# One-token attention: scores as rows with the query columns as weights, two value tiles in one accumulator, and 20 wide output rows

## The chip, the core and the metric

The kernel runs on one core of a Trainium2 chip. Its engines work side by side and wait for each other only through semaphores: TensorE (PE, with its weight loads listed as PEld), VectorE (DVE), ScalarE (ACT), GpSimd (POOL), and SyncE (SP), which here only issues transfers. PE writes into PSUM, a small memory of eight banks of 128 partitions x 512 f32 values; the other data lie in SBUF (128 partitions). The metric is the device time in microseconds of one execution. The kernel before took 189.35 us (median of 3 runs, 189.26 to 189.45).

## The reference

One token `x` (512 values) goes through two branches, mixed by a gate:

```python
g = sigmoid((x * gate_w).sum(-1))
# branch A: attention, 32 heads, 4096 cached keys and values of 128 values each
q = (x @ wq) as 32 heads of 128
p = softmax(einsum("hd,hkd->hk", q, k_cache) * 128 ** -0.5)
a = einsum("hk,hkd->hd", p, v_cache).reshape(4096) @ wo      # wo: 4096 x 512
# branch B: an MLP with 1376 hidden units
b = relu(x @ w1 + b1) ** 2 @ w2 + b2
out = g * a + (1 - g) * b                                     # 512 values
```

Everything is bf16. Keys and values are 33.6 MB each, wq and wo 4.2 MB each, w1 and w2 1.4 MB each: 78.3 MB that are read once.

## The kernel before

**Tiles.** Four heads make a tile; there are `NQ` = 8 tiles. A key tile is loaded as 128 partitions of 128 keys: partitions 32h to 32h+31 hold head h of the four, each partition 128 consecutive keys of its head. A value tile has the same layout. Three buffers hold keys (`Kt`), two hold values (`Vt`); the last two value tiles go into key buffers, wo into a value buffer.

**Transfers.** All large ones are issued by SP, in one queue and in this order: wq, K0, w1, w2, K1, V0, K2, K3, V1, K4, V2 and so on to V6, V7, and wo in four pieces of 20, 8, 3 and 1 rows (`TS`; a row is 128 of the 4096 inputs times 512 outputs). Where a buffer is used again the issue waits for its last reader: K2 goes where w1 and w2 were and waits for the MLP's last product (`s_ml`, line 258); K3 on waits for the transposes (`s_t`), DVE's products (`s_mu`) and POOL's products (`s_pm`) of an older tile; values wait for the value products (`s_pv`). The output leaves at the end.

**Scores.** The 128 keys in each partition of a tile are shared out among three engines:

- 68 go to POOL, in four pieces of 17 (line 310): keys times the query, which lies broadcast in `qb`, into `pg` (two buffers); DVE sums each piece (`psums`, line 691).
- 28 go to DVE alone, in two pieces of 14: `prods` (line 676) and `sums` (line 685).
- 32 go to PE, in four chunks of 8 (`TC`). `transposes(i, c)` (line 423) turns 8 blocks of 128x128 keys into a PSUM bank (`T`, three of them), `evac` on ACT (line 338) copies them to `kT`, and `scores(i, c)` (line 437) makes one product for each block: the turned keys are the weights, four query columns `qc` stream. PE issues the transposes two chunks ahead of the scores. At the end of a tile ACT copies the scores from `pS` into the score tile `Sb`, head by head (`score_copy`, line 344).

**Softmax of a tile.** DVE's `smax(i)` (line 698) takes the maximum of each partition, PE turns that column into a row (`max_rows`, 447), DVE's `gmax` (702) takes the maximum of each head, PE spreads it (`max_cols`, 451), ACT negates it (`neg_max`, 348) and makes the exponentials (`exps`, 355), which write `E`, four columns for each key block, zero outside the head's own partitions.

**Values.** `pv(i, a, b)` (line 466) makes 32 products for a tile: 16 columns of `E` (4 key blocks x 4 heads) are the weights and 4 x 128 value columns stream. They go round four column groups of the array, accumulators at partitions 0, 32, 64 and 96 of `pO`. After each tile `pv_copy` (ACT, line 361) copies 112 partitions of `pO` to `pvf`, and `extract(i)` (line 475) adds up what belongs to each head with the 0/1 matrix `pick`, into `O`.

**Order.** Each engine's order is written out by hand. PE, for tile i: transposes and scores of i; in tile 0 then the MLP (`mlp_h`, `mlp_c`, `mlp_out`); in tile 1 `mlp_cols`; then `max_rows(i-1)`, `extract(i-3)`, the first half of `pv(i-2)`, `max_cols(i-1)`, the second half. DVE, for tile i: `prods(i,0)`, `psums(i-1,3)`, `smax(i-1)`, `psums(i,0)`, `sums(i,0)`, `gmax(i-1)`, `psums(i,1)`, `prods(i,1)`, the next query, `psums(i,2)`, in tile 0 the MLP's two instructions (`mlp()`, lines 707 and 709), `sums(i,1)`.

**MLP.** `mlp_h` (lines 495 and 498) streams the bias and w1 (5 x 1376 columns) past one weight column into the three `T` banks; ACT copies the row (375); `mlp_c` (506) turns it into columns, and adds 1 to `s_h`, for which DVE's `mlp()` waits; `mlp_out` (516, 524) multiplies by w2.

**End.** After tile 7: `extract(5)`, `pv(6)`, `max_rows(7)`, `max_cols(7)`, `extract(6)`, then `busy(n)`: products whose result nobody uses, which fill PE's waits (line 569), two of them, one after each of three exponentials, the denominator (`den`, 482), five more, `pv(7)`, a copy by DVE (735), `extract(7)`, the scaling (738), `regroup` (537, 740), two more fillers, and the wo rows (`attn_rows`): 16 (`WW`) of the first piece's 20 are wide, 512 columns in four column groups of `pO` (547); DVE copies them to `pvf` (742), `wide_rows` (562) adds them up; the other rows are four products of 128 columns each (553).

Of the kernel before, what the change touches and what calls it, by code (L numbers as in the profile page):

```python
# [5 lines left out]
def bass_gated_mix__gqa_block_cached__dense_activation_squared_relu__decode_kernel(  # L6
# [21 lines left out]
    NH = 32  # L28
# [34 lines left out]
    NT = 3  # L63
    NR = 3
# [6 lines left out]
    WW = 16  # L71
# [12 lines left out]
    with ctx:  # L84
# [26 lines left out]
        xrow = sb("xrow", [1, DM], bf16)  # L111
        grow = sb("grow", [1, DM], bf16)
        b1r = sb("b1r", [1, F], bf16)
# [9 lines left out]
        pick = sb("pick", [128, 4, 60], fp32)  # L123
        pvf = sb("pvf", [112, 512], fp32)
        onesf = sb("onesf", [1, 128], fp32)
        qc = sb("qc", [128, NH], bf16)
        Sb = sb("Sb", [128, NS, NB], fp32)
        E = sb("E", [128, NE, NB, 4], bf16)
# [16 lines left out]
        b2r = Kt[0:1, 2, 14 * 1024:14 * 1024 + DM]  # L145
        b2g = Kt[0:1, 2, 15 * 1024:16 * 1024].bitcast(fp32)

        pick2 = sb("pick2", [112, 3], fp32)
# [13 lines left out]
        SL = pS[0:NH, 0:256].bitcast(bf16)  # L162
        H = pX[:, 160:160 + FN + TX]
# [9 lines left out]

        S = pS[:, 0:4 * max(YB)].rearrange("p (b h) -> p b h", h=4)

# [43 lines left out]
        s_sd = sem("s_sd")  # L219
        s_cp = sem("s_cp")  # L220
# [95 lines left out]
        def _(eng):  # L316
# [9 lines left out]
            for j in QA:  # L326
# [6 lines left out]
            eng.activation(qc[:, :].rearrange("p (j h) -> p j h", h=4), QT[:, :, 0:128:HP], ACT.Copy)\  # L333
               .then_inc(s_qc, 1)

            def evac(n):
                eng.wait_ge(s_t, n + 1)
                eng.activation(kT[:, n % NR, :], T[n % NT][:, :].bitcast(bf16), ACT.Copy).then_inc(s_ev, 1)  # L338
# [12 lines left out]
            def exps(j):  # L351
                eng.wait_ge(s_nm, j + 1)
                for h in range(4):
                    a, b = HP * h, HP * h + HP
                    eng.activation(E[a:b, j % NE, :, h], Sb[a:b, j % NS, :], ACT.Exp,  # L355
                                   bias=nM[a:b, 4 * j + h:4 * j + h + 1], scale=SCALE,
                                   accum_out=RS[a:b, 4 * j + h:4 * j + h + 1]).then_inc(s_e, 1)

            def pv_copy(j):
                eng.wait_ge(s_pv, j + 1)  # L360
                eng.activation(pvf[:, :], pO[0:112, :], ACT.Copy).then_inc(s_pc, 1)  # L361

            for i in range(NQ + 1):
                if i == NQ:
                    pv_copy(NQ - 3)
                    pv_copy(NQ - 2)
                if i < NQ:
                    for c in range(NC[i]):
                        evac(CB[i] + c)
                        if c == 1 and i >= 3:  # L370
                            pv_copy(i - 3)
                    score_copy(i)
                    if i == 0:
                        eng.wait_ge(s_h, 1)
                        eng.activation(hrow, TT[0:1, 0:F], ACT.Copy).then_inc(s_hw, 1)
                        eng.wait_ge(s_ml, 1)
                        eng.activation(pvf[:, :], pO[0:112, :], ACT.Copy).then_inc(s_mc, 1)
                if i >= 1:
                    neg_max(i - 1)
                    exps(i - 1)  # L380
# [4 lines left out]
        def _(eng):  # L385
# [29 lines left out]
            def transposes(i, c):  # L415
                n = CB[i] + c
                if c == 0:
                    eng.wait_ge(s_k[i % NK], 16 * (i // NK + 1))
                if n >= NT:
                    eng.wait_ge(s_ev, n - NT + 1)  # L420
                for y in range(TC):
                    w = XB[i] + c * TC + y
                    mm = eng.transpose(T[n % NT][:, :].bitcast(bf16)[:, y * 128:(y + 1) * 128],  # L423
                                       Kt[:, i % NK, w * 128:(w + 1) * 128], ident[:, :])
                mm.then_inc(s_t, 1)

            def scores(i, c):
                n = CB[i] + c
                eng.wait_ge(s_ev, n + 1)
                if c == 0:  # L430
                    if i == 0:
                        eng.wait_ge(s_qc, 1)
                        eng.wait_ge(s_g, 3)
                    else:
                        eng.wait_ge(s_cp, 4 * i)
# [19 lines left out]
            def pv(i, a, b):  # L455
                if a == 0:
# [5 lines left out]
                    if i >= 1:  # L462
                        eng.wait_ge(s_pc, i)
                for y in range(a, b):
                    r = 32 * (y % 4)
                    mm = eng.matmul(pO[r:r + 16, :], E[:, i % NE, 4 * y:4 * y + 4, :],  # L466
                                    VT(i)[:, y * 512:(y + 1) * 512], start=(y < 4), stop=(y >= NG - 4))
# [4 lines left out]
            def extract(i):  # L472
                eng.wait_ge(s_pc, i + 1)
                for b in range(4):
                    mm = eng.matmul(O, pick[0:112, b, 28 - 4 * i:60 - 4 * i], pvf[:, b * 128:(b + 1) * 128],  # L475
                                    start=False, stop=(i == NQ - 1 and b == 3), skip_group_check=True)
# [25 lines left out]
            def mlp_c():  # L502
                eng.wait_ge(s_hw, 1)
                eng.wait_ge(s_ho, 9)
# [4 lines left out]
            def mlp_out():  # L509
# [3 lines left out]
                eng.wait_ge(s_wm, 3)  # L513
# [14 lines left out]
            def mlp_cols():  # L528
                eng.wait_ge(s_mc, 1)
                for j in range(4):  # L530
                    eng.matmul(accs[j % 2], pick2[:, 1 - j // 2:3 - j // 2], pvf[0:112, j * 128:j * 128 + 128],
# [40 lines left out]
            for i in range(NQ):  # L572
                for c in range(NC[i]):
                    transposes(i, c)
                    if c >= 2:
                        scores(i, c - 2)
                scores(i, NC[i] - 2)
                scores(i, NC[i] - 1)
                if i == 0:
# [7 lines left out]
                if i >= 3:  # L587
                    extract(i - 3)
# [6 lines left out]
            extract(NQ - 3)  # L595
# [3 lines left out]
            extract(NQ - 2)  # L599
# [8 lines left out]
            extract(NQ - 1)  # L608
# [10 lines left out]
        def _(eng):  # L619
# [8 lines left out]
            eng.tensor_reduce(pick[:, :, 28:32],  # L628
                              identf[:, :].rearrange("p (c r) -> p c r", c=4)[:, :, 0:16]
                              .rearrange("p c (b h) -> p b h c", b=4), AX.X, ALU.add).then_inc(s_ho, 1)  # L630
# [3 lines left out]
            eng.wait_ge(s_ho, 7)  # L634
            eng.wait_ge(s_wm, 2)
            eng.tensor_copy(pick2[:, 1:2], pick[0:112, 0, 28:29]).then_inc(s_wm, 1)
# [98 lines left out]
            eng.tensor_copy(pvf[:, :], pO[0:112, :]).then_inc(s_pc, 1)  # L735
            eng.wait_ge(s_rd, 1)
            eng.wait_ge(s_ex, NQ)
# [4 lines left out]
            eng.tensor_copy(pvf[:, :], pO[0:112, :]).then_inc(s_wc, 1)  # L742
# [30 lines left out]
```

## Time and profile before

| what | value |
|---|---|
| runs (median of 3) | 189.35 us |
| span of the profiled execution | 188.1 us |
| median less span | 1.25 us |
| transfers | 78.48 MB, mean 417 GB/s |
| mean granted PE clock | 0.701 |
| one POOL piece (L310) | 4.32 us, 32 of them |
| DVE per tile: sums of POOL's pieces (L691), its own products (L676) and sums (L685) | 4 x 2.41, 2 x 2.01, 2 x 2.00 us |
| first key tile used by POOL, last POOL piece over | 22.8 us, 167.1 us |
| last wo piece issued, output issued | 151.0 us, 186.9 us |

The profile is one execution. Times in the time line are microseconds from the start of the span; a line gives start, duration, engine, line of the kernel, operation, output <- input, shapes, and in brackets the idle time before it and what ended that. The lines called windows give, for a stretch, the busy time of each engine (with the number of instructions), the granted PE clock (1.00 is full), the busy share of the transfer engines and their rate.

### The profile page before, as it was taken

Reading aid. Unit: us, or ns where it says so; the run is one execution under the profiler, and the core shown is the slowest. Engines: PE = TensorE matmul, PEld = TensorE weight load, DVE = VectorE, ACT = ScalarE, POOL = GpSimd, SP = SyncE. Lnnn points to the kernel's source line nnn. Section 1 sums busy time; section 2 is a strip of 40 time slices with the busy share of each in tenths; the row PEclk is TensorE's granted clock in tenths of the full one; section 3 lists DMA queues with packets and bytes.
Section 4 is the critical chain, followed back from the end, with each engine's and each line's share of the span. In section 5 each row is a group of like instructions: output and inputs, shape, how many; then the busy total and the mean of one; then the engine's idle time right before and its main releaser. Section 6 shows DMA issues by size and latency. Waiting matters only on the chain. (4 is left out here: it accounts for less than half of the span.)

```text
span 188.1 us, 2610 instructions
## 1 busy us (share of the span) xinstructions
PE 109.1 (58%) x1076; PEld 65.3 (35%) x1078; DVE 153.0 (81%) x127; ACT 69.6 (37%) x170; POOL 137.8 (73%) x38
## 2 busy tenths in 40 slices
PE   1129877788302839147506571758185649458986
PEld 0113253428202716133403171418141634214334
DVE  5122569999997999999999999999999999992022
ACT  2102476208320819403920573055405460505000
POOL 1000199998995999989998999899899989950000
PEclk9999999555755756657955866555855556755799
DMA  6999899999999999999999999999999999999993
GB/s 223 447 446 446 380 440 446 432 439 432 429 441 432 413 425 429 432 439 439 429 418 432 432 432 429 439 439 418 425 436 432 432 432 432 442 411 420 433 393 124
DMA packets 3374, 78.48 MB, mean 417 GB/s; under 512 B 394, under 2 KB 527, under 8 KB 676
## 3 DMA queue, kind: packets, MB, share of 16 engines
q1 hardware_dynamic: 3356, 78.32, 97.4%
q8 instruction: 8, 0.13, 0.3%
q14 instruction: 2, 0.02, 0.0%
q10 hardware_dynamic: 8, 0.01, 0.0%
HBM read 78.33 MB, written 0.00 MB: 416 GB/s over the span
## 5 line engine op out<-in xcount | busy, mean ns | idle before, releaser
L310 POOL TENSOR_TENSOR pg<-Kt,qb 128x2176 f32<-128x2176 bf16 x32 | 137.1, 4318 | 28.5 <-DMA Kt<-in_A_k_cache_dram 23.6
L691 DVE TENSOR_REDUCE Sb<-pg 128x17 f32<-128x2176 f32 x32 | 77.0, 2405 | 1.7 <-POOL pg L310 1.7
L338 ACT ACTIVATE kT<-T 128x1024 bf16<-128x1024 bf16 x32 | 30.8, 1030 | 16.7 <-PE T L423 16.5
L423 PE MATMUL T<-ident,Kt 128*128 128x128 bf16 x256 | 25.6, 280 | 18.2 <-DMA Kt<-in_A_k_cache_dram 18.2
L676 DVE TENSOR_TENSOR pr<-Kt,pQ 128x1792 f32<-128x1792 bf16 x16 | 32.2, 2011 | 2.1 <-DMA Kt<-in_A_k_cache_dram 1.3
L685 DVE TENSOR_REDUCE Sb<-pr 128x14 f32<-128x1792 f32 x16 | 32.1, 2004 | 0.0
L423 PEld LDWEIGHTS T<-ident,Kt 128*128 128x128 bf16 x256 | 22.4, 130 | 22.8 <-DMA Kt<-in_A_k_cache_dram 21.1
L466 PE MATMUL pO<-Vt,E 128*16 128x512 bf16 x192 | 21.8, 543 | 0.2 <-issue 0.2
L348 ACT ACTIVATE nM<-pM 128x4 f32<-128x4 f32 x8 | 1.4, 173 | 47.5 <-PE pM L451 47.5
L355 ACT ACTIVATE E<-Sb,nM 32x128 bf16<-32x128 f32 x32 | 18.6, 580 | 0.9
L437 PE MATMUL pS<-qc,kT 128*128 128x4 bf16 x256 | 11.7, 167 | 10.2 <-ACT kT L338 9.9
L475 PE MATMUL pX<-pvf,pick 112*32 112x128 f32 x64 | 14.5, 403 | 2.4 <-ACT pvf L361 2.4
L447 PE MATMUL pM<-identf,mp 128*1 128x128 f32 x8 | 2.8, 347 | 20.3 <-DVE mp L698 20.3
L437 PEld LDWEIGHTS pS<-qc,kT 128*128 128x128 bf16 x256 | 9.9, 102 | 12.3 <-ACT kT L338 12.2
L408 PE MATMUL T<-Vt,kT 128*128 128x512 bf16 x32 | 10.7, 484 | 3.4 <-DMA Vt<-in_A_wq_dram 3.4
L475 PEld LDWEIGHTS pX<-pvf,pick 112*32 112x32 f32 x64 | 9.5, 161 | 6.1 <-ACT pvf L361 2.9
L330 ACT ACTIVATE qb<-T 32x128 bf16<-32x128 f32 x20 | 5.4, 268 | 10.5 <-PE T L408 10.2
L663 DVE CAST qb<-T 32x128 bf16<-32x128 f32 x12 | 3.4, 287 | 6.5 <-PE T L408 6.2
L466 PEld LDWEIGHTS pO<-Vt,E 128*16 128x16 bf16 x192 | 6.4, 104 | 6.2 <-issue 4.0
L451 PE MATMUL pM<-gm,onesf 1*128 1x4 f32 x16 | 4.1, 325 | 7.4 <-DVE gm L702 7.2
L447 PEld LDWEIGHTS pM<-identf,mp 128*1 128x1 f32 x8 | 0.6, 79 | 21.8 <-DVE mp L698 21.6
L355 ACT ACTIVATION_READ_ACCUMULATOR E<-Sb,nM 32x1 f32 x32 | 8.1, 254 | 0.0
(81 smaller groups left out, 76.8 us busy)
## 6 DMA issues: line engine op xcount, KB each, us to landing
Kt<-in_A_k_cache_dram SPq DMA_DIRECT2D x8, 4096.0 KB, 31.0
Vt<-in_A_v_cache_dram SPq DMA_DIRECT2D x6, 4096.0 KB, 31.3
Kt<-in_A_v_cache_dram SPq DMA_DIRECT2D x2, 4096.0 KB, 31.3
Vt<-in_A_wq_dram SPq DMA_DIRECT2D x1, 4096.0 KB, 12.3
Vt<-in_A_wo_dram SPq DMA_DIRECT2D x1, 2560.0 KB, 32.9
Kt<-in_B_w_dram SPq DMA_DIRECT2D x1, 1376.0 KB, 24.4
Kt<-in_B_w_dram SPq DMA_DIRECT2D x1, 1280.0 KB
Vt<-in_A_wo_dram SPq DMA_DIRECT2D x1, 1024.0 KB, 34.9
```

The lines of the kernel that those rows point to most:

```text
L310: eng.tensor_tensor(pg[:, n % 2, 0:g, :], Kt[:, i % NK, k * g * 128:(k + 1) * g * 128] .rearrange("p (b d) -> p b d", b=g), qb[:, i:i + 1, ...
L330: eng.activation(qb[a:b, j, :], T[j % NT][a:b, h * 128:(h + 1) * 128], ACT.Copy)\
L338: eng.activation(kT[:, n % NR, :], T[n % NT][:, :].bitcast(bf16), ACT.Copy).then_inc(s_ev, 1)
L355: eng.activation(E[a:b, j % NE, :, h], Sb[a:b, j % NS, :], ACT.Exp, bias=nM[a:b, 4 * j + h:4 * j + h + 1], scale=SCALE, accum_out=RS[a:b, ...
L408: mm = eng.matmul(T[j % NT][:, :], xb[:, t, :], wq_sb[:, t, j * 512:(j + 1) * 512], start=(t == 0), stop=(t == 3))
L423: mm = eng.transpose(T[n % NT][:, :].bitcast(bf16)[:, y * 128:(y + 1) * 128], Kt[:, i % NK, w * 128:(w + 1) * 128], ident[:, :])
L437: mm = eng.matmul(S[:, c * TC + y, :], kT[:, n % NR, y * 128:(y + 1) * 128], qc[:, 4 * i:4 * i + 4], start=True, stop=True)
L466: mm = eng.matmul(pO[r:r + 16, :], E[:, i % NE, 4 * y:4 * y + 4, :], VT(i)[:, y * 512:(y + 1) * 512], start=(y < 4), stop=(y >= NG - 4))
L475: mm = eng.matmul(O, pick[0:112, b, 28 - 4 * i:60 - 4 * i], pvf[:, b * 128:(b + 1) * 128], start=False, stop=(i == NQ - 1 and b == 3), ski ...
L676: eng.tensor_tensor(pr[:, 0:x, :], Kt[:, i % NK, a * 128:(a + x) * 128] .rearrange("p (b d) -> p b d", b=x), PQ[:, i % 4:i % 4 + 1, :].bro ...
L685: eng.tensor_reduce(Sb[:, i % NS, a:a + x], pr[:, 0:x, :], AX.X, ALU.add).then_inc(s_sd, 1)
L691: eng.tensor_reduce(Sb[:, i % NS, k * g:(k + 1) * g], pg[:, n % 2, 0:g, :], AX.X, ALU.add)\
```

## The change

Four edits, which share the freed memory.

*Scores as rows.* In place of 8 products a chunk with the keys as weights there are two: 32 columns of a query matrix are the weights and 512 turned keys stream. The matrix `qw` holds the four query columns of a tile among zeros, and a window of 32 columns slid by four puts the scores of the u-th group of 512 keys into rows 4u to 4u+3 of one 32x512 accumulator (`SR`). ACT copies that to `srow`, PE turns it back with four f32 transposes (`score_rows`) into the third `T` bank, and ACT copies it to `Sb` as before. The transposes of the keys have two banks left (`NK2`), and PE issues them one chunk ahead. `mlp_h`, which uses the third bank, waits for the copies of tile 0.

*Value products of two tiles.* `E` has 32 columns for each product: an even tile fills the first 16, an odd one the last 16, zeros in the rest. Two tiles accumulate into the same `pO`, so `pv_copy` and `extract` come once for two tiles; `pick` and `pvf` grow to 128 partitions. `extract(6)` is gone from the end.

*wo.* `WW` becomes 20: all rows of the first piece are wide.

*Memory.* `xrow`, `grow`, `b1r`, `b2r` and `b2g` move into buffers that are free at that time; memsets of `E` and `qw` grow.

```diff
-    WW = 16
+    WW = 20
+    TG = 512 // 128
+    PW = 24
...
+        SR = pS[0:32, :]
+        ST = T[2][:, 0:128].rearrange("p (c u h) -> p c u h", c=TG, u=8)
...
-            eng.activation(qc[:, :].rearrange("p (j h) -> p j h", h=4), QT[:, :, 0:128:HP], ACT.Copy)\
-               .then_inc(s_qc, 1)
+            eng.wait_ge(s_wm, 3)
+            eng.activation(qw[:, :, 28:32], QT[:, :, 0:128:HP], ACT.Copy).then_inc(s_qc, 1)
...
             def score_copy(i):
-                eng.wait_ge(s_sc, CB[i + 1])
+                eng.wait_ge(s_sc, i + 1)
+                eng.activation(srow[:, :], SR, ACT.Copy).then_inc(s_rc, 1)
+                eng.wait_ge(s_bk, i + 1)
                 for h in range(4):
                     a, b = HP * h, HP * h + HP
-                    eng.activation(Sb[a:b, i % NS, XB[i]:NB], S[a:b, 0:YB[i], h], ACT.Copy).then_inc(s_cp, 1)
+                    eng.activation(Sb[a:b, i % NS, XB[i]:NB].rearrange("p (u c) -> p u c", c=TG),
+                                   ST[a:b, :, :, h].rearrange("p c u -> p u c"), ACT.Copy).then_inc(s_cp, 1)
...
-                for y in range(TC):
-                    mm = eng.matmul(S[:, c * TC + y, :], kT[:, n % NR, y * 128:(y + 1) * 128],
-                                    qc[:, 4 * i:4 * i + 4], start=True, stop=True)
-                mm.then_inc(s_sc, 1)
+                for g in range(TC // TG):
+                    u = c * (TC // TG) + g
+                    mm = eng.matmul(SR, qw[:, i, 28 - 4 * u:60 - 4 * u], kT[:, n % NR, g * 512:(g + 1) * 512],
+                                    start=(u == 0), stop=(u == 7))
+                if c == NC[i] - 1:
+                    mm.then_inc(s_sc, 1)
+
+            def score_rows(i):
+                eng.wait_ge(s_rc, i + 1)
+                if i >= 1:
+                    eng.wait_ge(s_cp, 4 * i)
+                for c in range(TG):
+                    mm = eng.transpose(T[2][:, 32 * c:32 * c + 32], srow[:, c * 128:(c + 1) * 128],
+                                       identf[0:32, 0:32])
+                mm.then_inc(s_bk, 1)
...
-                    mm = eng.matmul(pO[r:r + 16, :], E[:, i % NE, 4 * y:4 * y + 4, :],
-                                    VT(i)[:, y * 512:(y + 1) * 512], start=(y < 4), stop=(y >= NG - 4))
+                    mm = eng.matmul(pO[r:r + 32, :], E[:, i % NE, y, :], VT(i)[:, y * 512:(y + 1) * 512],
+                                    start=(y < 4 and i % 2 == 0), stop=(y >= NG - 4 and i % 2 == 1))
...
             def mlp_h():
                 eng.wait_ge(s_w1, 16)
                 eng.wait_ge(s_b, 16)
+                eng.wait_ge(s_cp, 4)
...
                     transposes(i, c)
-                    if c >= 2:
-                        scores(i, c - 2)
-                scores(i, NC[i] - 2)
+                    if c >= 1:
+                        scores(i, c - 1)
                 scores(i, NC[i] - 1)
+                score_rows(i)
...
-                if i >= 3:
-                    extract(i - 3)
+                if i >= 4 and i % 2 == 0:
+                    extract(i // 2 - 2)
...
             max_cols(NQ - 1)
-            extract(NQ - 2)
```

More of the change, by code (lines that the diff above doesn't have):

```diff
@@ L63, in bass_gated_mix__gqa_block_cached__dense_activation_squared_relu__decode_kernel @@
     NT = 3
+    NK2 = 2
     NR = 3
@@ L110, in bass_gated_mix__gqa_block_cached__dense_activation_squared_relu__decode_kernel @@
         WX = Kt[0:QX, 2, 4 * F + FN * DM:4 * F + (FN + TX) * DM]
-        xrow = sb("xrow", [1, DM], bf16)
-        grow = sb("grow", [1, DM], bf16)
-        b1r = sb("b1r", [1, F], bf16)
+        xrow = kT[0:1, 2, 0:DM]
+        grow = kT[0:1, 2, DM:2 * DM]
         ob = kT[:, 1, 0:256]
@@ L369, in _ @@
                         evac(CB[i] + c)
-                        if c == 1 and i >= 3:
-                            pv_copy(i - 3)
+                        if c == 1 and i >= 4 and i % 2 == 0:
+                            pv_copy(i // 2 - 2)
                     score_copy(i)
@@ L594, in _ @@
                     pv(i - 2, NG // 2, NG)
-            extract(NQ - 3)
+            extract(NQ // 2 - 2)
             pv(NQ - 2, 0, NG)
@@ L607, in _ @@
             busy(3)
-            extract(NQ - 1)
+            extract(NQ // 2 - 1)
             busy(1)
```

84 lines of the change are left out of this document (46 added, 38 removed).

## The prediction

> **What bounds the kernel now.** I read the page first, then the time line of SP's issues, of VectorE and GpSimd, and last the clock by stretches.
>
> ```profile
> span 188.1 us, 2610 instructions
> PE 109.1 (58%) x1076; PEld 65.3 (35%) x1078; DVE 153.0 (81%) x127; ACT 69.6 (37%) x170; POOL 137.8 (73%) x38
> ...
> PEclk9999999555755756657955866555855556755799
> DMA  6999899999999999999999999999999999999993
> ```
>
> The transfers are busy in every slice but the first and the last: 78.5 MB at some 430 GB/s fill the span. So nothing can end before the wo rows have landed. But DVE (VectorE) and POOL are a second chain of almost the same length: from the first key tile at 22.8 us to 167.1 us POOL hardly pauses, and DVE reduces what it makes. I look for the place where the change touches that chain.
>
> ```profile
> 35.88 2.41 DVE L691 TENSOR_REDUCE Sb<-pg 128x17 f32<-128x2176 f32 x1
> 38.21 0.22 DVE L707 TENSOR_SCALAR hr<-pX,omg 128x15 f32<-128x15 f32 x1
> ...
> 38.56 2.01 DVE L685 TENSOR_REDUCE Sb<-pr 128x14 f32<-128x1792 f32 x1
> ...
> 42.63 2.41 DVE L691 TENSOR_REDUCE Sb<-pg 128x17 f32<-128x2176 f32 x1
> ...
> 45.13 12.84 POOL L310 TENSOR_TENSOR pg<-Kt,qb 128x2176 f32<-128x2176 bf16 x3 [0.59 <-DVE Sb L691]
> ...
> 59.84 2.02 DVE L676 TENSOR_TENSOR pr<-Kt,pQ 128x1792 f32<-128x1792 bf16 x1 [1.28 <-DMA Kt<-in_A_k_cache_dram]
> ```
>
> The MLP's two instructions (L707, L709) stand in the middle of DVE's tile 0. Their input, the MLP's hidden row turned into columns by PE, is done at 36.18+1.87 = 38.05, and DVE reaches them at 38.2: no wait, and only 0.15 us of cover. What comes later than that stops DVE, then POOL (0.59 us waiting already at 45.13). The only place where DVE gets it back is the 1.28 us before tile 2's keys at 59.84; from there it runs at 18.0 us a tile (smax at 64.28, 82.28, 100.28 and on) without a gap.
>
> ```profile
> 175.63 0.27 PE L482 MATMUL pM<-onec,RS 128*32 128x1 f32 x2
> ...
> 177.06 1.90 PE L466 MATMUL pO<-Kt,E 128*16 128x512 bf16 x32
> ...
> 182.53 0.53 PEld L547 LDWEIGHTS pO<-Vt,o2p 128*1 128x1 bf16 x16 [0.47 <-DMA Vt<-in_A_wo_dram]
> ```
>
> The end: the last exponentials (tile 7) end at 174.26, the last value products start at 177.06, o2 is there at 181.90, two filling products later (182.56) the first wo rows are multiplied, landed at the same moment. So the attention chain has 177.06-174.26 = 2.8 us, of which the denominator (0.27) and five fillers (1.1 to 2.2, at 0.215 and 0.43 each) are spent in order: 0.4 to 1.4 us of real slack.
>
> **The change, part by part.**
>
> *Tile 0, before the MLP.* PE ran the MLP's first products at 30.62, right behind the last scores, while ACT copied the scores (0.82, L344). Now mlp_h waits for these copies, and they come after three more steps. (a) With two transpose buffers PE goes transposes, scores, transposes in turn. At full clock 8 transposes are 0.61 (first start to last end, 91.48) and two score products of 512 columns are 2 x 0.26 (four wide products in 1.03 at 21.11): 1.12 against ACT's 0.94 per evacuation. The last evacuation moves from 30.3 to 30.8, its two score products end at 31.4 instead of 30.7: +0.7. (b) The copy srow, 32x512: 0.60 (the 112x512 copy of L377). (c) Four f32 transposes: 15 small f32 ones take 1.87 (36.18), so 4 x 0.125, with the hand-overs 0.7. (d) The four copies, 0.82 as before, and a hand-over. mlp_h starts at about 33.65, +3.0.
>
> ```profile
> core 0: us, PE busy (x) PEld busy (x) DVE busy (x) ACT busy (x) POOL busy (x), PEclk, DMA share, GB/s
> 29.00:32.00 3.00, 2.01 (x23) 1.00 (x24) 3.00 (x3) 2.04 (x6) 3.00 (x2) 1.00 1.04 450
> 32.00:36.00 4.00, 2.79 (x10) 0.80 (x8) 4.00 (x4) 1.18 (x1) 4.00 (x2) 0.58 0.99 422
> 36.00:40.00 4.00, 3.13 (x27) 2.26 (x31) 3.97 (x4) 0.13 (x1) 3.92 (x1) 0.50 0.99 426
> ```
>
> (e) The granted clock falls to half at 32.6 us. Half of mlp_h was done by then; now all comes behind it. It streams 5 x 1376 = 6880 columns; at 0.43 per 512 that is 5.8 us, before it took 30.62 to 34.79 = 4.2. So +1.6. (f) A score product uses 32 weight columns, the transposes 128, so the next weights may not be loaded ahead. PEld stands 0.85 before the transposes at 41.99, after such a change; bounds 0 to 0.85 a time, two times on this path and two in tile 1. I take 0.1 each, since the transposes in question run at both clocks and the 0.85 has a wide product at half clock in it: 0.2 here.
>
> [...]
>
> The sum is 3.0+1.6+0.2 = 4.8; less the cover, DVE stands about 4.6. [...]
>
> *Tile 1.* Behind mlp_out PE takes tile 1, then max_rows(0), for which DVE waits at gmax (49.59, now 54.2). Before, its transposes and scores went from 42.00 to 47.2. Now from 46.8, at half clock to begin with (8 transposes 0.91, two scores 0.86), one chunk costs 1.8 against 0.94; with the clock full from 49.7 (it changes here at 46.25, 49.67, 63.29, 66.74, always whole multiples of 3.41 apart) I get the scores at 53.0, srow 53.7, turned back 54.4, mlp_cols (0.60) 55.0, max_rows 55.4: DVE stands 1.2 more, and 0.2 for the changes of width. Bounds 0 (full clock) and 3.4 (half clock to the end). Later tiles: the same work takes up to 10 us, between gmax(i-1) and gmax(i) lie 18, less 3 for max_cols and the value half; PE's own lateness is covered there. If it were not, DVE would stand again.
>
> *DVE's account.* 4.6+1.4-1.28 = 4.7 us late from tile 2 on, and so at the last exponentials: 174.26 becomes 179.0. POOL follows DVE.
>
> *The transfers.* SP issues K2, K3 and V1 after mlp_out (42.09, now 46.8). The first ten slices have moved 19.4 of the 19.6 MB issued before, so the mean queue runs dry near 47.4; V0 lands about 49.9 (K1 at 40.2 plus 9.7 a tile). From issue to the first bytes 1.6 us (0.73 at the start, and 223 of some 440 GB/s in the first 4.7 us). So a gap of about 1 us in the early queues, none in the late ones, whose landing counts. It would lie behind the later chain at the end. V2 and later are issued with 16 us queued ahead; 5 us less is covered.
>
> *Value products.* Still 32 a tile, with 32 columns: the 16-column ones load in 0.09 beside the product; nothing. Half of the copies (0.60) and extractions (1.9) go; ACT and PE were not the bound there: nothing. But extract(6), 171.54 to 173.46, kept PE busy ahead of the fillers. The clock rose at 175.96, after a stretch of 3.41 with 3.07 busy. The same stretch now holds some 2.8, and such ones have both risen (2.66 at 107.7) and not (2.73 at 117.95). If it does not rise until 182.8, the fillers and the first half of the last value products run at half: 1.7 us. I take 0.8 of bounds 0 and 1.7.
>
> *End.* 179.0 + denominator 0.3 + fillers 1.3 = 180.6; from the start of the value products to the first wo rows 5.5 (177.06 to 182.56): 186.1, plus 0.8 = 186.9. From there it took 188.1-182.56 = 5.54. Of 20 rows in column groups the last is 1.29 behind the first (16 took 1.03), the copy and wide_rows wait for it, and rows 16 to 19 no longer fill that copy: +0.25. End of span 192.7. Around the span lie 189.35-188.1 = 1.25 in the median of the runs: 194.0 (193.9 to 194.1 by the rounding).
>
> *Start.* Larger memsets on DVE (E twice, one more reduction, qw: about 1.0 us in all by L631 and L628) end before 5 us; DVE waits for xrow until 7.75: hidden. If that cover were gone the q products would still wait for wq at 13.1.
>
> **Rivals.**
>
> *The clock stays full past 32.6.* Wide scores are heavier work than 4-column ones. Then mlp_h is done at 36.9, DVE stands 1.9, tile 1 costs nothing, 0.6 us remain, and the 0.4 to 1.4 of slack at the end hide them: only the 0.25 of wide_rows and up to 0.8 of clock: 189.6 to 190.4, say 189.8. For it: it stayed full at 29.2 after a stretch with gaps. Against: it fell at 32.64 although PE was busier there than it will be.
>
> *The clock stays halved through tile 1.* DVE stands 3.4 there instead of 1.4: 196.0. For it: mlp_out kept PE busy from 39.7 to 42.1 and the clock did not rise at 42.8. Against: it rose at 46.25 after nothing but transposes and scores. [...]
>
> *Faster: the transfers speed up.* The place is the SBUF: 256 score weight loads of 128 columns become 64 of 32. If transfers had waited for such reads, one per cent of their 182 us is 1.8: 187.5. It decides only if DVE is late by less than 1.4 us too. Against: GB/s is 426 with PE at work (43 to 46) and about 430 while PE stands (52 to 58).
>
> *The change does not take effect*: the diff alters the order on PE itself, so I give this nothing beside the others.
>
> **How the numbers follow.** Forecast (DVE late by some 3 to 6.5 us: 192 to 196) 0.68; full clock 0.15; halved clock or worse 0.12; transfers 0.05. The range 190.2 to 196.6 leaves out faster, most of the full clock and the far end of the halved one. A difference of 0.2% (0.4 us) is what a measurement can tell. Faster 0.05; same 0.09, from the full clock; slower 0.86, its rest and the two late cases.
>
> **What would show it.** A wait of DVE at the MLP's two instructions of 3.5 to 6 us, released by PE; a second one at gmax(0); tile 2's keys without a wait; smax every 18.0 us from there but 4 to 5 us later; SP's issue of K2 at 46 to 47; the last exponentials at 178 to 180; and the wo rows waiting for o2, not for a transfer. I am wrong if DVE's wait is under 2 us, if PE's tile time makes DVE stand in every tile, or if the wo rows still start at 182.5.

## The result and the profile after

The changed kernel takes 192.68 us (median of 5 runs, 191.58 to 195.26) against 189.45 for the kernel before (5 runs, 189.26 to 189.51). The ratio is 1.015, 95% interval 1.0126 to 1.0174: slower by 3.2 us, where 4.65 were predicted. A second set of 6 runs gave 192.83 and 1.0181 (1.0154 to 1.0208). The medians are of all runs; the ratios, here and below, use the runs within 1.5% of the fastest of their kernel, which leaves out the one of 195.26.

The runs of the changed kernel lie 3.7 us apart, those of the kernel before 0.25. The profiled execution of the first set is the longest of its five (195.26); the one of the second set, called the second profile here, is the shortest of its six (191.93). They are read side by side, for the difference between them is the key to the rest.

The first profile's page:

```profile
span 193.8 us, 2218 instructions
...
PEclk9999978585795585975588797657958695557599
DMA  6999999998999999999999999999999999999940
GB/s 230 427 433 440 421 457 435 433 429 345 372 423 433 436 426 433 433 440 436 426 433 433 433 433 416 433 433 433 433 433 423 433 433 433 433 436 390 418 173 4
```

The transfers now thin out in the last two slices (before: in the last alone), so something else sets the end. The dip in the tenth and eleventh slices (345 and 372 GB/s, at 44 to 53 us) stands where K2 was issued late. VectorE's time line in the same profile (start, duration, line, and in brackets the wait and its releaser):

```profile
35.81 2.41 DVE L715 TENSOR_REDUCE Sb<-pg 128x17 f32<-128x2176 f32 x1
43.84 0.23 DVE L731 TENSOR_SCALAR hr<-pX,omg 128x15 f32<-128x15 f32 x1 [5.62 <-PE pX L529]
...
56.10 0.28 DVE L726 TENSOR_REDUCE gm<-pM 1x4 f32<-1x128 f32 x1 [0.78 <-PE pM L469]
...
65.21 2.02 DVE L700 TENSOR_TENSOR pr<-Kt,pQ 128x1792 f32<-128x1792 bf16 x1
```

DVE stands 5.62 us before the MLP (it came to it at 38.2, as before) and 0.78 at gmax(0). At tile 2's keys it no longer waits: the 1.28 us of cover are used up. smax(1), which stands in DVE's tile 2 and is called "smax of tile 2" in the expectations below, comes at 69.65 instead of 64.28. The next ones follow at 18.0 us as before, and smax(7) comes at 175.30 instead of 169.93: DVE is 5.4 us late to the end. TensorE's time line shows why, first profile:

```profile
33.12 0.43 PE L459 MATMUL T<-identf,srow 32*128 32x32 f32 x4 [0.68 <-ACT srow L349]
34.55 1.30 PE L518 MATMUL T<-Kt,ident 1*1 1x512 bf16 x3 [1.00 <-ACT Sb L353]
35.78 4.75 PE L521 MATMUL T<-Kt,xcol 128*1 128x512 bf16 x12
...
188.30 1.25 PE L570 MATMUL pO<-Vt,o2p 128*1 128x512 bf16 x20
```

and the same places in the second profile, with DVE's two waits:

```profile
33.83 0.74 PE L518 MATMUL T<-Kt,ident 1*1 1x512 bf16 x3 [1.01 <-ACT Sb L353]
34.49 2.48 PE L521 MATMUL T<-Kt,xcol 128*1 128x512 bf16 x12
...
185.02 1.25 PE L570 MATMUL pO<-Vt,o2p 128*1 128x512 bf16 x20
```

```profile
40.28 0.23 DVE L731 TENSOR_SCALAR hr<-pX,omg 128x15 f32<-128x15 f32 x1 [1.80 <-PE pX L529]
...
53.63 0.28 DVE L726 TENSOR_REDUCE gm<-pM 1x4 f32<-1x128 f32 x1 [1.87 <-PE pM L469]
```

The MLP's products start at nearly the same time (34.55 and 33.83, before 30.62), behind the copy of the rows, the turning back and the copies of the scores. But the twelve products of w1 take 4.75 us in one execution and 2.48 in the other. The windows show the granted clock (the column after POOL's), first profile and then second:

```profile
32.00:36.00 4.00, 2.32 (x10) 0.64 (x9) 4.00 (x4) 1.34 (x5) 4.00 (x2) 0.73 1.06 459
36.00:40.00 4.00, 4.00 (x11) 1.28 (x10) 2.22 (x1) 0.00 (x0) 4.00 (x2) 0.50 0.97 414
40.00:44.00 4.00, 2.41 (x17) 1.79 (x15) 0.16 (x1) 1.31 (x1) 4.00 (x1) 0.92 0.96 410
44.00:48.00 4.00, 3.61 (x27) 1.06 (x28) 3.83 (x4) 0.26 (x1) 0.09 (x1) 0.51 0.91 393
```

```profile
36.00:40.00 4.00, 2.60 (x17) 1.97 (x16) 2.49 (x2) 1.31 (x1) 4.00 (x1) 0.94 1.01 430
40.00:44.00 4.00, 3.42 (x29) 0.85 (x29) 3.55 (x4) 0.00 (x0) 3.81 (x2) 0.50 0.95 410
44.00:48.00 4.00, 3.74 (x27) 2.53 (x26) 3.91 (x4) 2.54 (x3) 1.42 (x2) 0.50 1.05 451
```

Windows of 1 us place the changes. In the first profile the clock is halved from 33.8 to 40.6, over all of w1's products, full until 44.0, and halved again to 50.9. In the second it is full until 39.5 and halved to 49.8. So mlp_out and the first half of tile 1 run at half clock in both; the MLP's products do so in the first alone. The waits follow. The first is 5.62 or 1.80 us. The second hangs on PE's way from the turned hidden row (over at 43.80 and 40.24) to gmax(0): of its 12.3 us in the first profile the half clock covers 6.8, of its 13.4 in the second 9.5, and the wait is 0.78 or 1.87. In all DVE waits 6.40 or 3.67 us; smax(1) is 5.37 or 2.91 us late, and the first wo rows come 5.76 or 2.48 us after the 182.54 of before. In both they wait for o2, not for a transfer: wo's first piece had landed at 154.96+29.8 = 184.8 and 152.50+30.2 = 182.7 (issue and duration of its transfer; before 149.61+32.9 = 182.5).

The mean granted clock, which was taken for every run, sorts the eleven runs of the changed kernel into three groups: three at 0.776 took 191.58 to 192.04 us, five at 0.768 or 0.769 took 192.44 to 193.04, three at 0.751 to 0.753 took 193.23 to 195.26. The spread goes with the clock; which stretch was halved is known for the two profiled runs only, and the runs of e11 below are not sorted in this way.

### The profile page after: what moved, and what is told of

It is laid out like the page before. It is cut to its first block, busy times and chain, and to the rows that moved or that the text cites. A ratio compares the mean times of both kernels' runs of the same rounds, so it can differ in the third digit from the quotient of the medians.

```text
span 193.8 us, 2218 instructions
## 1 busy us (share of the span) xinstructions
PE 122.0 (63%) x874; PEld 57.0 (29%) x874; DVE 153.9 (79%) x129; ACT 73.4 (38%) x174; POOL 137.7 (71%) x38
## 5 line engine op out<-in xcount | busy, mean ns | idle before, releaser
L345 ACT ACTIVATE kT<-T 128x1024 bf16<-128x1024 bf16 x32 | 31.9, 1023 | 14.4 <-PE T L434 14.1
L449 PE MATMUL pS<-kT,qw 128*32 128x512 bf16 x64 | 23.4, 454 | 8.0 <-ACT kT L345 7.7
L434 PEld LDWEIGHTS T<-ident,Kt 128*128 128x128 bf16 x256 | 20.7, 123 | 21.6 <-issue 8.8
L488 PE MATMUL pO<-Vt,E 128*32 128x512 bf16 x192 | 21.8, 578 | 0.0
L419 PE MATMUL T<-Vt,kT 128*128 128x512 bf16 x32 | 9.5, 445 | 3.3 <-DMA Vt<-in_A_wq_dram 3.3
L449 PEld LDWEIGHTS pS<-kT,qw 128*32 128x32 bf16 x64 | 3.7, 97 | 16.5 <-ACT kT L345 15.1
L488 PEld LDWEIGHTS pO<-Vt,E 128*32 128x32 bf16 x192 | 6.2, 122 | 6.4 <-issue 5.2
L473 PEld LDWEIGHTS pM<-gm,onesf 1*128 1x128 f32 x16 | 3.1, 244 | 16.0 <-DVE gm L726 16.0
L353 ACT ACTIVATE Sb<-T 32x32 f32<-32x32 f32 x32 | 6.0, 188 | 4.7 <-PE T L459 4.2
L497 PE MATMUL pX<-pvf,pick 128*32 128x128 f32 x32 | 6.8, 385 | 1.5 <-ACT pvf L373 1.5
## 6 DMA issues: line engine op xcount, KB each, us to landing
Vt<-in_A_wq_dram SPq DMA_DIRECT2D x1, 4096.0 KB, 12.3
Vt<-in_A_wo_dram SPq DMA_DIRECT2D x1, 2560.0 KB, 29.8
```

The lines of the kernel that those rows point to most:

```text
L345: eng.activation(kT[:, n % NR, :], T[n % NK2][:, :].bitcast(bf16), ACT.Copy).then_inc(s_ev, 1)
L419: mm = eng.matmul(T[j % NT][:, :], xb[:, t, :], wq_sb[:, t, j * 512:(j + 1) * 512], start=(t == 0), stop=(t == 3))
L434: mm = eng.transpose(T[n % NK2][:, :].bitcast(bf16)[:, y * 128:(y + 1) * 128], Kt[:, i % NK, w * 128:(w + 1) * 128], ident[:, :])
L449: mm = eng.matmul(SR, qw[:, i, 28 - 4 * u:60 - 4 * u], kT[:, n % NR, g * 512:(g + 1) * 512], start=(u == 0), stop=(u == 7))
L473: eng.matmul(MB[:, 4 * i:4 * i + 4], onesf[:, :], gm[:, 4 * i:4 * i + 4], start=True, stop=True) .then_inc(s_mb, 1)
L488: mm = eng.matmul(pO[r:r + 32, :], E[:, i % NE, y, :], VT(i)[:, y * 512:(y + 1) * 512], start=(y < 4 and i % 2 == 0), stop=(y >= NG - 4 an ...
```

## The experiments

They ran in this order. The first four take the change apart, the next four look for what in the late MLP costs the time, the last three settle it. Each is compared with the kernel before on its own chip (189.40 to 189.51).

### e1: the MLP before the turning back

The MLP's first part goes ahead of the turning back of tile 0's scores, and ACT's copy of its row stands right behind srow. All else is as changed.

```diff
             def mlp_h():
-                eng.wait_ge(s_cp, 4)
...
-                score_rows(i)
                 if i == 0:
                     mlp_h()
                     mlp_c()
+                score_rows(i)
+                if i == 0:
                     mlp_out()
```

> The changed kernel, with the MLP's first products and the turning of its row put ahead of the turning back of tile 0's scores (ACT copies the hidden row right after srow), so that the MLP no longer waits for the score copies. Theory (the late MLP stops DVE): mlp_h starts some 2.1 us earlier than in the changed kernel (the copy of srow, the four transposes and the four copies leave its path, 34.55 against 32.45 in that profile), DVE's wait at the MLP falls from 5.6 by the same 2.1, and so does the time: 192.7 to 190.6. Rival (the loss sits at the end: the missing extraction, the clock, the wide rows): unchanged, 192.0 to 193. Rival (transfers run dry because K2 is issued late): K2 is issued 2.1 earlier too, so the time falls, but DVE's later tiles would show waits for keys.

Measured: 189.42 us (11 runs), ratio 0.9998 (0.999 to 1.0007). PE, DVE and the end:

```profile
32.23 2.48 PE L521 MATMUL T<-Kt,xcol 128*1 128x512 bf16 x12
...
38.24 0.22 DVE L732 TENSOR_SCALAR hr<-pX,omg 128x15 f32<-128x15 f32 x1
...
50.66 0.28 DVE L727 TENSOR_REDUCE gm<-pM 1x4 f32<-1x128 f32 x1 [0.96 <-PE pM L470]
...
182.37 1.25 PE L570 MATMUL pO<-Vt,o2p 128*1 128x512 bf16 x20 [0.50 <-DMA Vt<-in_A_wo_dram]
```

DVE reaches the MLP at 38.24 without a wait, and the wo rows wait for their transfer again, at 182.37. The whole loss is gone, more than was expected of this run (190.6). The expectation went by the 5.62 of the first profile; here w1's products run at full clock (2.48), and K2 is issued on time too (41.51). Which of the two makes up the difference was not tested. At gmax(0) DVE still waits 0.96 us, since tile 1 takes PE longer with the scores as rows (8.94 us from its first transposes to max_rows(0), before 5.74), but that lies within the 1.28 us before tile 2's keys, and smax(1) comes at 64.22. So the scores as rows cost no time anywhere else, in none of the eight tiles: the place of the MLP is the loss. wo landed at 149.53+32.8 = 182.3, within 0.2 us of before: the rival that fewer weight loads speed the transfers up is out.

### e2: the kernel before with a late MLP

```diff
             def mlp_h():
+                eng.wait_ge(s_ps, 2)
                 eng.wait_ge(s_w1, 16)
```

> The kernel before, with one wait more: mlp_h waits until DVE has summed POOL's second piece of tile 0 (33.84 in the profile of before, against its start at 30.62). Nothing else is changed. Theory (the late MLP alone makes most of the loss): 3.2 later, plus 1.6 because all of it now lies behind the fall of the clock at 32.6: DVE stands 4.7 at the MLP, 1.28 of it comes back at tile 2's keys, 3.4 are left at the last exponentials, of which 0.4 to 1.4 are hidden: 191.5 to 192.5. Rivals (the loss is in the tile work of PE, the value products or the end): 189.4, as before.

The wait is for DVE's sum of POOL's second piece. Measured: 192.13 us, ratio 1.015 (1.0129 to 1.0171), as its theory had it, and about as much as the change loses, without anything else of it. The w1 products took 4.75 us here as well:

```profile
43.04 0.23 DVE L708 TENSOR_SCALAR hr<-pX,omg 128x15 f32<-128x15 f32 x1 [4.89 <-PE pX L507]
...
184.95 1.03 PE L548 MATMUL pO<-Vt,o2p 128*1 128x512 bf16 x16 [0.37 <-DMA Vt<-in_A_wo_dram]
```

The way is not quite that of the changed kernel. DVE stands only at the MLP (4.89) and not at gmax(0); smax(1) comes 3.70 us late, near the 4.89 less the cover of 1.28. K2 is issued at 46.93, and at the end the wo rows wait 0.37 us for their transfer, not for o2: the two ways in which a late MLP can cost, DVE and the landing of wo, are nearly level here (184.6 and 184.9).

### e3 and e4: the other parts alone

e3 is the kernel before with 20 wide rows; e4 is the changed kernel with the old scores and 16 wide rows, so that only the value products of two tiles and the moved small buffers are left of the change.

```diff
-    WW = 16
+    WW = 20
```

> The kernel before with 20 wide wo rows in place of 16 and nothing else. Theory: rows 16 to 19 no longer fill the copy of the accumulators, 0.25 more: 189.7. Rival (fewer products at the end help): 189.2 or less.

> The changed kernel with the scores of before (keys as weights, three transpose buffers, no turning back, no wait of the MLP for the copies) and 16 wide wo rows: what is left of the change is the value products of two tiles in one accumulator, with extract(6) gone, and the moved small buffers. Theory: DVE is not late; the end loses what the clock costs after extract(6) is gone, between 0 and 1.7: 189.4 to 190.4, most likely 189.8. Rival (the end makes the loss): 191 or more.

Measured: e3 189.35 us, 0.9998 (0.9989 to 1.0007); e4 189.40 us, 1.0000 (0.9991 to 1.0009). Neither costs or brings anything. In e3 the 20 rows stand at the landing of wo, at 182.43, and the end behind them is no later than with 16: the +0.25 for the wide rows is not there.

### e5: DVE takes the MLP later

DVE's two MLP instructions go behind the last sum of tile 0, which gives them 2.0 us more.

```diff
-                    if i == 0:
-                        mlp()
                     sums(i, 1)
+                    if i == 0:
+                        mlp()
```

> The changed kernel with DVE's two MLP instructions put behind its last sum of tile 0 (2.0 us of work that does not need them). PE's order, and so the issue of K2, stays as it is. Theory A (the late MLP costs through DVE's wait alone): DVE is late by 2.0 less, and every run by 2.0 less: 192.4 to 190.4. Theory B (the late MLP costs on two ways at once, through DVE's wait and because K2 is issued 5 us late and the transfers run dry): DVE gains 2.0, but the wo rows still land some 2.4 late (184.9 in the run with the late MLP in the kernel before): 191.6, and the spread of the runs shrinks. Theory C (the transfers alone): 192.4 unchanged.

Measured: 193.01 us (191.43 to 195.37), ratio 1.0169 (1.0123 to 1.0214): nothing won. The time is that of Theory C, but its reason is another than the transfers. DVE's two waits, in an execution whose clock changes within 0.5 us of where the first profile's did from 30 to 52 us:

```profile
43.75 0.23 DVE L731 TENSOR_SCALAR hr<-pX,omg 128x15 f32<-128x15 f32 x1 [3.55 <-PE pX L529]
...
56.19 0.28 DVE L726 TENSOR_REDUCE gm<-pM 1x4 f32<-1x128 f32 x1 [3.08 <-PE pM L469]
```

The first wait shrank from 5.62 to 3.55, and the second grew from 0.78 to 3.08; gmax(0) stands at 56.19, as in the changed kernel (56.10). PE does tile 1's transposes, scores, turning back and mlp_cols between the MLP and max_rows(0): that chain sets gmax(0), and a DVE that is earlier by 2 us before it only waits longer there.

### e6, e7 and e8: the transfers

K2 is issued after the MLP, so it is late too. e7 makes it late alone, in the kernel before; e6 issues the first half of K3, whose buffer is free earlier, ahead of K2 in the changed kernel, so that the queue does not run dry; e8 is e6 and e5 together.

e7:

```diff
                     eng.wait_ge(s_ml, 1)
+                    eng.wait_ge(s_ps, 5)
```

e6:

```diff
             def load_k(i):
+                if i == 2:
...
+                    eng.dma_start(Kt[:, 0, 0:8192], k_p[384:512, 0:8192]).then_inc(s_k[0], 16)
...
+                if i == NK:
+                    eng.dma_start(Kt[:, 0, 8192:16384], k_p[384:512, 8192:16384]).then_inc(s_k[0], 16)
+                    return
```

> The changed kernel with the first half of K3 issued ahead of K2 (it waits only for tile 0's readers, about 40 us), so that the queue has 2.1 MB more when K2 is issued late; DVE's wait at the MLP stays. Theory A and B (DVE's wait is enough by itself): the transfers keep 430 GB/s through 45 to 52 us, wo lands near 182.5, and the time is still 191.5 to 192.7. Theory C (the transfers alone): 189.4.

> The kernel before with one wait more on SP: K2 waits until DVE has summed the first POOL piece of tile 1 (47.75 us in the profile of before), which is when the changed kernel issued it (47.74). The MLP is as early as before. Theory B: the transfers run dry, everything behind lands 2.4 late, tile 2's keys too, and the time is 191.5 to 192. Theory A (as predicted: the gap is in the early queues only and lies hidden): 189.4 to 189.8.

> The two edits together in the changed kernel: DVE's MLP instructions 2.0 later in its order, and half of K3 ahead of K2. Theory B: both ways are eased, DVE's end is 2.0 earlier than in the changed kernel and the transfers no longer hold it: 190.0 to 190.6. Theory A: the same as with DVE's edit alone, 190.4. Theory C: 189.4.

Measured: e7 191.54 us, ratio 1.012 (1.010 to 1.014); e6 194.66 us, 1.0273 (1.026 to 1.0286); e8 194.42 us, 1.0249 (1.022 to 1.0278). In e7 K2 is issued at 47.92 instead of 42.09:

```profile
61.45 2.02 DVE L677 TENSOR_TENSOR pr<-Kt,pQ 128x1792 f32<-128x1792 bf16 x1 [2.81 <-DMA Kt<-in_A_k_cache_dram]
...
184.21 1.03 PE L548 MATMUL pO<-Vt,o2p 128*1 128x512 bf16 x16 [0.56 <-DMA Vt<-in_A_wo_dram]
```

This is what Theory B had. The gap reaches the end: wo lands 1.7 us later and its rows wait for it; DVE loses 1.6 at tile 2's keys. The median is 2.1 us longer. In e6 the queue stayed full (414 and 446 GB/s in the slices from 43 to 53 us) and wo landed at 154.70+28.1 = 182.8, but the kernel became slower by 2 us, outside all that was expected, since tile 2's keys now stood behind half of K3:

```profile
64.96 2.02 DVE L708 TENSOR_TENSOR pr<-Kt,pQ 128x1792 f32<-128x1792 bf16 x1 [2.68 <-DMA Kt<-in_A_k_cache_dram]
```

So e6 is no test of the transfers alone. What it does show: with wo on time the wo rows still came at 187.55, five microseconds after they could. DVE's lateness sets the end here, not the landing of wo; but 2.68 us of that lateness come from the keys, so e6 does not say what sets the end of the changed kernel. There the two profiles say it: the wo rows wait for o2. e8's time lies outside all three of its theories too (wo at 182.6, rows at 188.04, a wait of 4.03 us at gmax(0) and of 0.94 at the keys).

### e9 to e11: both waits of DVE, one by one

If e5 won nothing because gmax(0) was next, both have to be taken away. e9 is the changed kernel again (its profile is the second one above). e11 moves max_rows(0) on PE from behind all of tile 1 to behind the transposes of its third chunk; e10 does that and what e5 does.

```diff
                     transposes(i, c)
+                    if i == 1 and c == 2:
+                        max_rows(0)
                     if c >= 1:
                         scores(i, c - 1)
...
-                if i >= 1:
+                if i >= 2:
                     max_rows(i - 1)
```

> The changed kernel once more, unchanged, for a second profile and as the neighbour of the next run. Theory (the late MLP costs a sum of DVE's wait and PE's late tile 1, both stretched or not by where the clock's changes fall, with the late K2 as a floor): a profile whose span lies below the first one's 193.8 must show the clock rising earlier after tile 0 or falling later: DVE waits less than 5.62 at the MLP or gmax(0), or the last value products take less than 2.97; never is the first wo row before 184.5, since wo lands some 2 us late with K2 issued at 46 to 48. Median 191.6 to 193.2. Rival (the spread is the transfers'): the DVE waits and the products of the first profile come again to 0.2 us and only the landing of wo moves.

> The order of e5 (DVE takes the MLP after the last sum of tile 0) and on PE max_rows(0) moved from behind tile 1's whole chain to behind the third chunk's transposes of tile 1. Theory (in e5 nothing was won because tile 1's chain on PE kept gmax(0) at 56.2): gmax(0) comes at about 53 without a wait, DVE is 3 us earlier; then the late K2 decides: DVE waits for tile 2's keys again, to about 61.5, smax of tile 2 ends at 65.9 to 66.5, and the end is the landing of wo or at most 1 us later: median 191.2 to 192.0. Rival (the attention chain is late for another reason, such as POOL or the copies on ACT): gmax(0) comes earlier, but smax of tile 2 stays at 69 or later and the median within 0.4 of e5's 193.0.

> The changed kernel with only max_rows(0) moved behind the third chunk's transposes of tile 1; DVE keeps its order. This is the fourth corner beside the changed kernel (192.8), e5 (193.0) and e10 (189.8). Theory (DVE stands twice in series, at the MLP by 1.8 to 5.6 us and at gmax(0) by what PE is late beyond that, and each of the two edits of e10 takes away one of them): gmax(0) without a wait, smax of tile 2 later than the 64.28 of before by the MLP's wait less 1.3, that is 0.5 to 4.3 us, and after the 0.5 us of slack at the end a median of 189.6 to 193.0, with 190.8 in the middle: some half of the 3.4 us. Rival (the wait at gmax(0) alone is the loss, the MLP's wait is always within it): 189.4 to 189.9, as e10. Second rival (the two edits only work together, since smax(0) is held up by the MLP as long as max_rows(0) is by tile 1): 192.4 to 193.2.

Measured (median us; ratio to before with its interval):

| | max_rows(0) after tile 1 | max_rows(0) inside tile 1 |
|---|---|---|
| DVE takes the MLP before its last sum | e9 192.83; 1.0181 (1.0154 to 1.0208) | e11 190.57; 1.0057 (1.0039 to 1.0074) |
| DVE takes the MLP after it | e5 193.01; 1.0169 (1.0123 to 1.0214) | e10 189.76; 1.0017 (1.0007 to 1.0028) |

The profile of e11 has the same clock over the MLP as the second profile, so they can be laid side by side. DVE and the end in e11:

```profile
40.08 0.23 DVE L733 TENSOR_SCALAR hr<-pX,omg 128x15 f32<-128x15 f32 x1 [1.83 <-PE pX L529]
...
51.48 0.27 DVE L728 TENSOR_REDUCE gm<-pM 1x4 f32<-1x128 f32 x1
...
182.52 1.25 PE L570 MATMUL pO<-Vt,o2p 128*1 128x512 bf16 x20 [0.31 <-DMA Vt<-in_A_wo_dram]
```

The first wait is the same (1.80 and 1.83), the second is gone, gmax(0) stands at 51.48 instead of 53.63, smax(1) at 65.02 instead of 67.19, and the wo rows wait for their transfer as before. This execution took 189.40 us, the second profile's 191.93. The other runs of e11 reach up to 193.36: where the half clock falls on the MLP the first wait should be the long one (none of these runs has a profile), and the median lies at 190.57, near the middle of what was expected (190.8). e10 takes that away too:

```profile
40.72 0.23 DVE L733 TENSOR_SCALAR hr<-pX,omg 128x15 f32<-128x15 f32 x1 [0.69 <-PE pX L529]
...
49.99 0.27 DVE L728 TENSOR_REDUCE gm<-pM 1x4 f32<-1x128 f32 x1
...
59.81 2.02 DVE L702 TENSOR_TENSOR pr<-Kt,pQ 128x1792 f32<-128x1792 bf16 x1 [0.85 <-DMA Kt<-in_A_k_cache_dram]
...
182.88 1.25 PE L570 MATMUL pO<-Vt,o2p 128*1 128x512 bf16 x20 [0.50 <-DMA Vt<-in_A_wo_dram]
```

Here w1's products took 3.77 us, the clock rising amid them (at 36.3); DVE waits 0.69 us at the MLP, nowhere else before tile 2's keys, and there it is back on the time of before (59.81, before 59.84). What is left is 182.88 against 182.54 at the wo rows, which wait for their transfer, and 0.34 us in the median. That fits the late K2 (issued at 44.62), though no run takes K2's lateness away here. e10's expectation put it at 2 us, after e7; but e7 had issued K2 3.3 us later still.

e9's own theory is borne out where it speaks of the waits (1.80 is well below 5.62) and of the end (185.02, above 184.5), but not in its reason for the latter: wo had landed at 182.7.

## Why the prediction was right, and where it was off

**The place and the mechanism were right.** In both profiles DVE waits for PE at the MLP's two instructions and again at gmax(0), tile 2's keys come without a wait, smax follows every 18.0 us, and the wo rows wait for o2. e1 and e2 show the place from both sides: without the late MLP the loss is gone, and the late MLP alone loses about as much (2.7 us of 3.2). e10 shows that it is DVE's waits and not PE's lateness as such: PE begins tile 1 as late (44.52, in the second profile 44.08), and 0.34 us remain of 3.4.

**The sizes were right for one run and not for the other.** The signs that the prediction named were a first wait of 3.5 to 6 us, smax 4 to 5 us later, K2 issued at 46 to 47 and the last exponentials at 178 to 180. The first profile has 5.62, 5.37, 47.74 and 179.23; the second has 1.80, 2.91, 44.17 and 177.07. A first wait under 2 us was one of its signs of being wrong, and the second profile shows it: there the wait at gmax(0) (1.87), which the prediction took for the small one, is the larger. It is still a wait for the same late PE.

**Terms before the MLP.** mlp_h was put at 33.65 and started at 34.55 and 33.83. The steps (a) to (d) hold: srow took 0.59 (0.60), the four copies 0.82, the hand-overs 0.5 to 1.0 each. The upper bound of (f), 0.85 at each change of width, would have put mlp_h at some 35.3 (two of them, 1.7, on top of 33.65); the 33.83 leaves no room for it. In the first profile the weight loads of the transposes stand 0.42 us behind two score products at full clock and 0.84 at half clock, but the transposes start 0.54 us (51.34 to 51.88) and 0.96 us (49.79 to 50.75) behind the first of the two products, 0.02 and 0.10 more than the 2 x 0.26 and 2 x 0.43 of the products alone: no more than the 0.1 of (f). The 34.55 is the first profile's, where the clock was halved from 27.0 to 30.4 as well.

**The mis-sized term: the half clock under the MLP, (e).** The prediction let the MLP run at half clock (wait 4.6) and tile 1 partly so too (1.4), 6.0 in all. Measured are 6.40 in the longest run, close to it, and 3.67 in a short one. For tile 1 it had the clock right: full from 49.7, measured 50.9 and 49.8. What it took for settled was the clock under the MLP, and that differs from run to run. The median of 192.7 lies between; no profile of a run right at it was taken. The 189.8 of the rival "the clock stays full past 32.6" came true only by half: in the second profile the clock is full through the MLP, and DVE's wait is the 1.80 that this rival had (1.9). But it went on to say that tile 1 costs nothing then. The clock fell at 39.5 instead, tile 1 cost 1.87, and the run took 191.93. With that wait removed, e11's execution of the same clock took 189.40, near the rival's time. The rival that the clock stays halved through tile 1 came in neither profile.

**Two waits in series.** The prediction adds them. In e5, 2.07 us less of the one came back as 2.30 more of the other: gmax(0) hangs on PE alone. The sum was right for the change as it is, but it does not say what either wait is worth by itself: DVE's order alone wins nothing (193.01), PE's order alone 2.3 us (190.57), and DVE's another 0.8 on top of it (189.76).

**The transfers.** "None in the late ones, whose landing counts" was wrong: wo landed 2.3 us late in the first profile and 0.2 in the second, and a late K2 by itself cost 2.1 us in e7, at tile 2's keys and at wo. That it would lie behind the later chain at the end was right in both profiles. K2 was put at 46.8; it was issued at 47.74 and 44.17. One reading under the rival of faster transfers does not hold for its whole stretch: from 43 to 46 us the kernel before moves 404 GB/s, not 426, and from 52 to 58 it moves 438. That is no ground against the rival; e1 is.

**The end, and luck.** The prediction's last steps can be laid beside both profiles (us; each column adds up to the end of the span):

| step | before | predicted | first profile | second profile |
|---|---|---|---|---|
| last exponentials end | 174.25 | 179.0 | 179.23 | 177.07 |
| from there to the last value products | 2.81 | 1.6 | 2.56 | 2.51 |
| from there to the first wo rows | 5.48 | 6.3 | 6.51 | 5.44 |
| from there to the end of the span | 5.55 | 5.8 | 5.51 | 5.51 |
| end of the span | 188.1 | 192.7 | 193.8 | 190.5 |

The second row was mis-sized: the prediction let 1.2 us of the lateness vanish in the slack before the last value products, and only 0.25 to 0.3 did. The five fillers there took 2.31 and 2.26 us (before 1.30), as five at 0.43 each would (2.15). The third row holds the 0.8 for the missing extract(6). It came in the first profile, as value products at partly half clock (1.90 before, and 1.91 in the second), and not in the second:

```profile
181.79 2.97 PE L488 MATMUL pO<-Kt,E 128*32 128x512 bf16 x32
```

The 0.25 for the wide rows, in the fourth row, was not there (e3). So the 194.0 came within 1.3 us of the median partly by luck: too much slack was taken off, and in the second profile too much lateness and too much at the end were put on. No profile of a run at the median shows how the terms fall there.

**Nothing won.** The fewer instructions on PE (874 products and 874 weight loads, before 1076 and 1078) buy no time, as predicted; ACT has four more (174) and is busy for 73.4 us instead of 69.6. e1, with all of it and the MLP in its old place, ties at 0.9998. Its wo rows wait for their transfer, and so do those of the kernel before. No version tried was faster than the kernel before.

## What to carry to other kernels

When an edit delays one small step, follow every reader of it to the next wait on the same engine: two waits in series that hang on one late producer can cover each other, so that removing one shows nothing until the other goes too (in e5, 2.07 us less of the first were 2.30 more of the second), and a table of both, each and neither says so at once. When the slack is under a microsecond, price each step on the late chain at both clocks, and read a second profile before you call either price the right one: the one step that the prediction took to run at half clock did so in one run and not in another (4.75 and 2.48 us). And an issue that slips behind the point where its queue runs dry can cost at the end (1.7 us at the landing of wo in e7), so read the time of issue beside the landing.

## What the runs showed of the hardware

The runs of one kernel on the same data lay 2% apart, and the granted clock differed with them (0.776 in the shortest, 0.753 in the longest). The twelve w1 products took 2.48, 3.77 and 4.75 us (second profile, e10, first profile) though they began within 2.2 us of each other (33.64 to 35.78). The kernel before hid such differences behind its transfers (0.25 us between its five runs; in its 17 runs beside e9 the granted clock went from 0.682 to 0.746 and the time only from 189.25 to 189.73); the changed one has no slack there, and shows them (3.7 us). The clock's changes that the prediction lists from the profile of before lie 3.42, 13.62 and 3.45 us apart, those of the first profile (33.8, 40.6, 44.0, 50.9) 6.8, 3.4 and 6.9, those of the second (39.5, 49.8) 10.3: within 0.1 us whole multiples of 3.41 in these three executions. From one profile to another they are not: the fall at 39.5 us in the second lies 5.7 us behind the one at 33.8 in the first. What sets their place in a run, no run here shows.

K2's issue 5.8 us later, with nothing else changed (e7), cost 1.7 us at the landing of wo, over 130 us after the gap: what the queue lost there was not made up in the rest of the span.
